# Couples 4 to 8 of an attention and feed-forward kernel: whole filler products, reordered sums, a third place in PSUM

## The chip, the cores and the metric

One core of one Trainium2 chip. The metric is the device time of one execution in microseconds (us). TensorE does the matrix products, VectorE, ScalarE and GpSimd the element-wise work, SyncE issues most of the DMAs.

## The reference

Two blocks follow each other. The first is attention with normalised queries and keys, for 8 batches, 12 heads, 448 rows and a head dimension of 64:

```python
def rmsnorm(x, g):
    rms = np.sqrt(np.mean(x * x, axis=-1, keepdims=True) + 1e-06)
    return x / rms * g
q_n, k_n = (rmsnorm(q, g_q), rmsnorm(k, g_k))
scores = 1.0 / np.sqrt(q.shape[-1]) * np.matmul(q_n, k_n.transpose(0, 1, 3, 2))
scores = scores - np.max(scores, axis=-1, keepdims=True)
attn = np.exp(scores)
attn = attn / (np.sum(attn, axis=-1, keepdims=True) + 1e-09)
attn_out = np.matmul(attn, v)
...
h = x @ w_in
g = h * (1.0 / (1.0 + np.exp(-h)))
out = g @ w_out
```

Between them the heads are brought side by side: x has 3584 rows of 768. w_in is 768 x 2048, w_out 2048 x 768. All is computed in float32; the weights come as 64-bit words that the kernel rounds to float32 itself.

## The kernel before, in words

**Couples.** The attention is done in 24 couples (c = 0 to 23), each of two pairs of heads of one batch; six couples (GROUP) make two batches, whose x is then complete. The loop at L1596 calls visit(c) (L1428) and between(c) (L1504). visit(c) holds the scores of couple c (scores, L726: keys times queries on TensorE in four 64x64 tiles, then the exponential on ScalarE, L740, with the key's factor as its scale), the weighing of the values by the exponentials (weigh, L750), and the division of the couple before (divide, L832). The 448 keys are three full steps (j = 0, 1, 2) of 128 and 64 left over (LEFT). between(c) transposes the next couple's q and k on TensorE (L636, L657; from couple 9 on, VectorE does it, flip, L670), adds the exponentials up (add, L777, on VectorE; sum_up, L790, on TensorE by products with ones), and forms and spreads the reciprocals of the sums (L817 to L828, with two DMAs behind each other for each half).

From couple 6 on, the left-over exponentials of a couple take the place e[1][:, 0] (left_weights, L616), which the first addition add(c, 1) reads.

**Filler products.** The feed-forward block's products are laid into the stretches of the attention in which TensorE would wait. A block of two by two tiles is computed with seven products instead of eight (class Seven, L920). Each product is three matmuls of 128x448 (each of them two passes in the records) that accumulate in one PSUM bank; what follows it (a copy to SBUF on ScalarE, L942 and L952, or a sum on VectorE, L884) takes it out. Products 1 and 2 are in two(), products 6, 5, 7, 3, 4 in five(), in this order. All this is one Python generator that hands over after each matmul, and fill (L1364) draws from it, twice in each between(c): it adds a share of matmuls to filler["due"] and draws until nothing is due, dealing the pieces of other work (`others`: additions, rounding of weights, square sums) evenly between the matmuls, and those of `prompt` (reciprocals and so on) at every third. What follows a product is emitted when the generator is drawn from for the next matmul. The share is 2.4 matmuls in couples 3 to 5 (make_ahead, L973, begun at L1555: 12 matmuls over 5 fills; here the part after a product belongs to the same draw as its last matmul), 13 in couples 6 to 11, 14 after that.

**PSUM.** Eight banks: two single ones named "mm" (used in turn by products, and until couple 5 by sum_up), two tiles of two banks named "sc" (used in turn by each call of scores, by the transposes of q and of k, by sum_up from couple 6 on), and two "av" banks of the weighing. bank (L910) chooses where a product goes: with turns["third"] set and more than 5 matmuls due, every second product goes to an "sc" tile. turns["third"] is set between visit and between for couples from 8 on, and taken back after the first fill up to couple 10 (L1550, L1598).

```python
def bank(n):
    turn = turns["next"] = (turns["next"] + 1) % 4
    if turns["third"] and filler["due"] > 5 * S and not turns["aside"]:
        turns["aside"] = True
        return ps.tile([P, 2, BANK], F32, name="sc", bufs=2)[:, 0, 0:n]
```

**Other work of couples 5 to 7.** normalise(c) (L839) gives pieces: squares of q by ScalarE (L472), their sums by VectorE (L473), the inverse root by VectorE and GpSimd (L497, L501), the scaling of q by GpSimd (L516, at L858), and the same without a scaling for k. Couple 7's q pieces are dealt in couple 5's first fill, its k pieces in visit 6. sum_x (L1005) forms the sums of x that products 5, 6, 4 and 7 need: four steps for each of three parts c; in visit 6 all four steps of the parts 1 and 2 follow the division (L1461 to L1464). The weights are opened by ScalarE (open, L91: L103, L104) and rounded by VectorE and GpSimd (round, L108: L126, L129, L133, L137); sum_w_in (L986) forms the sums of the weights. At couple 10 (FULL, L558) the left-over exponentials are not added by VectorE but given to sum_up as one more term of four matmuls (L801).

**The second matrix.** After the couples, quads of row blocks go through the second product; deep (L1230) again uses seven products, and VectorE and ScalarE combine them.

Of the kernel before, what the change touches and what calls it, by code (L numbers as in the profile page):

```python
# [449 lines left out]
class Norm:  # L450
# [15 lines left out]
    def squares(self, rows, t, out, alone):  # L466
        nc, n = self.nc, out.shape[1]
        t = t[0 : rows.shape[0], 0 : rows.shape[1]]
        if alone:
            nc.vector.tensor_tensor(out=t, in0=rows, in1=rows, op=ALU.mult)  # L470
        else:
            nc.scalar.activation(t, rows, AF.Square)  # L472
        nc.vector.tensor_reduce(  # L473
            out=out, in_=t.rearrange("p (n d) -> p n d", n=n), axis=AX.X, op=ALU.add
        )
# [65 lines left out]
def bounded(  # L541
# [15 lines left out]
    SOON = 2 * GROUP - 1  # L557
    FULL = SOON - 1  # L558

# [230 lines left out]
    def sum_up(c):  # L790
# [8 lines left out]
        if early:  # L799
            terms = [(0, lambda: weights(c, LEFT - 1))] + terms + [(1, None)]  # L800
        if c == FULL:  # L801
            terms.insert(0, (1, None))
# [36 lines left out]
    def normalise(c):  # L839


        def piece(name, i):
            t = scratch[i if c < GROUP + 2 else 0]
            source = raw_of(c) if c < GROUP else q_of(c)
            if name == "q":
                norm.squares_q(c, source, t, i)
            else:
                norm.squares_k(c, place[z.BY_ROWS if c >= LATE else f"k{c % 2}"], t, i)
# [5 lines left out]
            elif i == 1:  # L854
                norm.root(c, name)
                if name == "q":
                    for m in range(2):
# [48 lines left out]
    ps_alone = None  # L906
    turns = dict(next=0, aside=False, third=False)
    filler = dict(work=iter(()), due=0.0, share=0.0)

    def bank(n):  # L910
        turn = turns["next"] = (turns["next"] + 1) % 4
        if turns["third"] and filler["due"] > 5 * S and not turns["aside"]:
            turns["aside"] = True
# [6 lines left out]
    class Seven:  # L920
# [10 lines left out]
        def product(self, name):  # L931
            t, ends = bank(self.n), (self.steps[0], self.steps[-1])
            for s in self.steps:
                nc.tensor.matmul(  # L934
                    t, self.left(name, s), self.right(name, s), start=s == ends[0], stop=s == ends[1]
                )
                if not (self.prompt and s == ends[1]):
                    yield self.n
            return t

        def two(self):
            nc.scalar.copy(self.p1, (yield from self.product("1")))  # L942
            if self.prompt:
                yield self.n
            plus((yield from self.product("2")), self.p1, self.done[1, 1])
            if self.prompt:
                yield self.n

        def five(self):
            p1, u2, u3, p5, done = self.p1, self.u2, self.u3, self.p5, self.done  # L950
            plus((yield from self.product("6")), p1, u2)
            nc.scalar.copy(p5, (yield from self.product("5")))  # L952
            plus((yield from self.product("7")), u2, u3)
            nc.gpsimd.tensor_tensor(out=u2, in0=u2, in1=p5, op=ALU.add)  # L954
            nc.gpsimd.tensor_tensor(out=done[2, 2], in0=u3, in1=p5, op=ALU.add)
            plus((yield from self.product("3")), u2, done[1, 2])
            plus((yield from self.product("4")), u3, done[2, 1])


# [76 lines left out]
    def halves_in(group, blocks, beside=lambda m: iter(()), begun={}, fetched=()):  # L1036
# [11 lines left out]
        for i, m in enumerate(blocks):  # L1048
# [5 lines left out]
            count = 0  # L1054
            for n in columns:
                count += 1
                if (count - 1) % HW == 0:
# [172 lines left out]
    def deep(name, out, more, following, then=lambda t, h: None):  # L1230
# [30 lines left out]
        then(0, 1)  # L1261
        sum_deep_left(following, (0, 1))
        plus(product(7), u2, u3)
        x = added(u3, out[1][0])
        plus(u3, added(p5, out[1][1]), out[1][1])
        then(1, 1)
# [97 lines left out]
    def fill(others=(), prompt=()):  # L1364
# [7 lines left out]
        while filler["due"] > 0:  # L1372
            step = next(filler["work"], None)
            if step is None:
                break
            filler["due"] -= step
            steps += 1
            if prompt and steps % HW == 0:
                prompt.pop(0)()
            while dealt < min(len(others), len(others) * steps // total):  # L1380
                others[dealt]()
                dealt += 1
        filler["due"] = min(filler["due"], 0.0)
        for other in prompt + others[dealt:]:
# [21 lines left out]
    for c in range(GROUP // 2):  # L1406
        halves[2 * (c - GROUP)], halves[2 * (c - GROUP) + 1] = "rr", "o"
    sums_halves = {-6: [(0, 0)], -4: [(0, 1)], -3: [(0, 2)], -2: [(0, 3)]}
    sums_halves[8] = [(3, 0), (3, 1)]
# [18 lines left out]
    def visit(c):  # L1428
# [17 lines left out]
        if c > 0:  # L1446
# [12 lines left out]
            else:  # L1459
                divide(c - 1, sums)  # L1460
                if c == GROUP:  # L1461
                    for steps in (range(2), range(2, 4)):
                        for i in range(1, HW):
                            sum_x(last_two(c), i, steps)  # L1464
                run_all(beside[1:2])
# [38 lines left out]
    def between(c):  # L1504
# [19 lines left out]

        if c == GROUP - 1:
            transposes_and_sums()
        if c < LATE - 1:
# [13 lines left out]
        late = add(c, LEFT - 1) if c >= GROUP else []  # L1541
        if c >= GROUP and c != FULL:
            late += add(c, LEFT)
        further = normalise(c + 2) if c >= GROUP - 1 else []
        late += weights_in(c, 0) + (further[2:] if c >= GROUP else further[:2])
        if LATE - 1 <= c < SOON:
            late.insert(len(late) // 2, lambda: load_q(c + 2))
        fill(late)
        if c < SOON:
            turns["third"] = False  # L1550
        prompt = transposes_and_sums() if GROUP // 2 <= c != GROUP - 1 else []
        if prompt and c < GROUP:
            prompt.insert(0, lambda: None)
        if c == GROUP // 2:
            begin(make_ahead([0, 1]), AHEAD * 2 * HW * S, GROUP - 1)  # L1555
        if c >= LATE - 2:
# [39 lines left out]
    for c in range(NC):  # L1596
        visit(c)
        turns["third"] = c >= LATE - 1  # L1598
        between(c)
    turns["third"] = False  # L1600
    visit(NC)
# [225 lines left out]
```

## Time and profile before

| | us |
|---|---|
| median of 3 runs (1309.18 to 1310.33) | 1309.45 |
| the profiled execution, its own time | 1311.17 |
| its span | 1309.4 |
| TensorE busy in the span | 1291.4 |
| VectorE busy | 951.8 |
| ScalarE busy | 502.7 |
| GpSimd busy | 363.9 |
| TensorE busy of 59 us, 68 to 127 (couples 4, 5, visit 6) | 56.42 |
| TensorE busy of 26 us, 127 to 153 (after visit 6) | 24.54 |
| TensorE busy of 34 us, 153 to 187 (couple 7) | 33.12 |
| TensorE busy of 35 us, 187 to 222 (couple 8) | 33.38 |
| TensorE busy of 40 us, 222 to 262 (couple 9, visit 10) | 39.76 |

The span runs from the first to the last instruction that the profiler recorded. A line of the timeline has the start, the duration from the first start to the last end, the engine, the line of the program, the operation, the names written and read, the shape, and the number of instructions merged. In square brackets stands the idle time of the engine before it and what ended it. A "waits" line has the total, the number of times and the longest. "PE" is TensorE, "DVE" VectorE, "ACT" ScalarE, "POOL" GpSimd; a "q" behind them is the engine's queue, in which DMAs are issued. Ends of matmuls are modelled, and their starts are records: the pace is read from starts.

visit(4) begins at 74.3 us, visit(5) at 96.5, visit(6) at 116.6, visit(7) at 152.2, visit(8) at 187.0, visit(9) at 221.6.

### The profile page before, as it was taken

To read this page: it belongs to the slowest core of one execution; us is meant where nothing else is said; L and a number is where in the kernel's file an instruction comes from. 1 tells how busy PE (TensorE), PEld (TensorE's weight loads), DVE (VectorE), ACT (ScalarE), POOL (GpSimd) and SP (SyncE) were. 2 spreads that over 40 slices of the span, in tenths; PEclk is the share of its full clock that TensorE was granted. 3 is DMA by queue.
4 is the path that set the end of the run, shared out by engine and by line. 5 is a ranking of instruction groups with operands and counts; after the bars stand their busy time and mean duration, and the time that the engine had idled before them with its cause. 6 is when DMAs were issued, how large, how long until landed. Compare 5 with 4: busy or idle time off the path is not lost.

```text
span 1309.4 us, 19898 instructions
## 1 busy us (share of the span) xinstructions
PE 1291.4 (99%) x7178; PEld 828.3 (63%) x7178; DVE 951.8 (73%) x1628; ACT 502.7 (38%) x880; POOL 363.9 (28%) x227
## 2 busy tenths in 40 slices
PE   8999999999999999999999999999999999999998
PEld 4334444444444444444444455558999999999998
DVE  6898767877655556755554786698978787878785
ACT  7866666655544555545544354310000000100000
POOL 6765545453334333334321244300000000000000
PEclk9999999999999999999999999999999999999999
DMA  8675346544444444444321457312323223231411
GB/s 230 167 191 140 93 105 174 144 100 122 97 94 92 123 94 93 99 114 94 86 67 61 142 189 253 125 61 80 105 82 101 90 90 108 71 127 52 135 42 40
DMA packets 267967, 146.32 MB, mean 112 GB/s; under 512 B 204356, under 2 KB 251748, under 8 KB 267860
## 3 DMA queue, kind: packets, MB, share of 16 engines
q1 hardware_dynamic: 267200, 143.80, 40.0%
q8 instruction: 59, 0.97, 0.3%
q0 software_dynamic: 352, 0.96, 0.2%
q14 instruction: 48, 0.39, 0.1%
q10 hardware_dynamic: 308, 0.20, 0.1%
HBM read 95.36 MB, written 41.29 MB: 104 GB/s over the span
## 4 chain that ended last, share of the span: by engine, by line
PE 78%; DVE 2%; ACT 1%; issue 1%; DMA 0%; SPq 0%; ACTq 0%; DVEq 0%
PE alone L1241 23%; PE mm L934 16%; PE sc L934 9%; PE mm L1241 8%; PE alone L934 7%; PE av L772 6%; PE sc L735 6%; PE alone L1278 2%; PE sc L810 1%; PE mm L1278 1%; ACT work L740 0%; DVE work L884 0%; DVE work L786 0%; DVE stage L884 0%; ACT L1579 0%
## 5 line engine op out<-in xcount | busy, mean ns | idle before, releaser
L740 ACT ACTIVATE work<-sc,rms 128x448 f32<-128x448 f32 x318 | 181.3, 634 | 72.9 <-PE sc L735 57.1
L934 PE MATMUL mm<-x,W 128*128 128x448 f32 x396 | 163.4, 546 | 4.7 <-DVE stage L884 1.7
L735 PE MATMUL sc<-work 64*64 64x448 f32 x1344 | 163.8, 544 | 1.4 <-ACT work L740 1.1
L786 DVE TENSOR_TENSOR work<-work 128x896 f32<-128x896 f32 (+1 forms) x112 | 122.5, 1124 | 50.3 <-PE av L772 49.8
L772 PE MATMUL av<-work,rows 64*64 64x448 f32 x1272 | 150.5, 540 | 1.4 <-DVE x L1450 0.9
L934 PE MATMUL mm<-sums_x,W 128*128 128x448 f32 x360 | 147.6, 543 | 1.0 <-DVE parts L884 1.0
L501 POOL TENSOR_TENSOR rms<-rms,minus_half 128x14 f32<-128x14 f32 (+4 forms) x40 | 95.7, 2394 | 135.1 <-DVE rms L497 131.1
L934 PEld LDWEIGHTS mm<-x,W 128*128 128x128 f32 x396 | 72.9, 190 | 85.8 <-issue 70.8
L528 POOL DMA_DIRECT2D out_dram<-x x2 | 1.2, 594 | 443.2 <-DVE x L884 443.2
L934 PEld LDWEIGHTS mm<-sums_x,W 128*128 128x128 f32 x360 | 67.0, 190 | 72.8 <-issue 67.0
L1241 PE MATMUL alone<-W,rows 128*128 128x192 f32 x610 | 113.0, 326 | 0.0
L772 PEld LDWEIGHTS av<-work,rows 64*64 64x64 f32 x1272 | 57.1, 132 | 70.7 <-issue 34.5
L1241 PEld LDWEIGHTS alone<-W,rows 128*128 128x128 f32 x610 | 101.4, 190 | 0.0
L735 PEld LDWEIGHTS sc<-work 64*64 64x64 f32 x1344 | 53.0, 132 | 71.7 <-ACT work L740 29.8
L711 POOL TENSOR_TENSOR rms<-rms,minus_half 128x28 f32<-128x28 f32 x15 | 71.9, 4794 | 67.3 <-DVE rms L708 60.9
L934 PE MATMUL sc<-x,W 128*128 128x448 f32 x216 | 87.9, 543 | 0.0
L954 POOL TENSOR_TENSOR parts<-parts,stage 128x448 f32<-128x448 f32 x31 | 41.5, 1339 | 148.3 <-DVE parts L884 147.9
L1241 PE MATMUL alone<-W,work 128*128 128x192 f32 x382 | 72.2, 326 | 0.0
L934 PEld LDWEIGHTS sc<-x,W 128*128 128x128 f32 x216 | 40.4, 190 | 42.9 <-issue 40.6
L1072 ACT ACTIVATE stage<-stage 128x896 f32<-128x896 f32 x63 | 57.3, 945 | 21.9 <-DVE stage L884 21.0
L1251 ACT COPY rows<-alone 128x192 f32<-128x192 f32 x33 | 10.5, 318 | 141.8 <-PE alone L1241 78.1
L1241 PEld LDWEIGHTS alone<-W,work 128*128 128x128 f32 x382 | 63.8, 190 | 0.0
(261 smaller groups left out, 2282.6 us busy)
## 6 DMA issues: line engine op xcount, KB each, us to landing
hidden<-stage SPq DMA_DIRECT2D x63, 448.0 KB, 3.1
work<-hidden SPq DMA_DIRECT2D x21, 1024.0 KB, 5.2
rows<-in_moe_w_out_dram SPq DMA_DIRECT2D x32, 384.0 KB, 3.3
W<-in_moe_w_in_dram SPq DMA_DIRECT2D x22, 512.0 KB, 5.1
x<-hidden SPq DMA_DIRECT2D x7, 1024.0 KB, 5.7
rows<-in_q_dram SPq DMA_DIRECT2D x120, 56.0 KB, 2.2
rows<-in_k_dram SPq DMA_DIRECT2D x120, 56.0 KB, 2.3
work<-work SPq DMA_DIRECT2D x111, 56.0 KB, 2.0
```

The costliest lines, as they stand in the source:

```text
L501: nc.gpsimd.tensor_tensor(out=t, in0=t, in1=half, op=ALU.pow)
L711: nc.gpsimd.tensor_tensor(out=f, in0=f, in1=minus_half.to_broadcast([P, n]), op=ALU.pow)
L735: nc.tensor.matmul(two[ds(half * D, D), h, 0:S], keys[rows, ts(half, D)], qT[rows, pair, :], start=True, stop=True,)
L740: nc.scalar.activation(left_weights(c)[:, h] if j == LEFT else weights(c, j)[:, i, h], two[:, h, 0:S], AF.Exp, scale=norm.column(c, i, h, j),)
L772: nc.tensor.matmul(sums[i][ds(h * D, D), :], v, w, start=(j == 0 and step == 1), stop=(j == LEFT - 1 and step == 1),)
L786: nc.vector.tensor_tensor(out=total, in0=total, in1=more, op=ALU.add)
L810: nc.tensor.matmul(t[ds(h * D + i * n, n), :], ones[:, which + i if which else 0], left_weights(c)[:, h] if which else w()[:, i, h], start ...
L934: nc.tensor.matmul(t, self.left(name, s), self.right(name, s), start=s == ends[0], stop=s == ends[1])
L954: nc.gpsimd.tensor_tensor(out=u2, in0=u2, in1=p5, op=ALU.add)
L1072: nc.scalar.activation(t, t, AF.Silu)
L1241: nc.tensor.matmul(t, x[:, i], y, start=i == ORDER[0], stop=i == ORDER[-1])
L1278: nc.tensor.matmul(o, a[:, 2 * i + m, t], right_one(name, i)[:, m], start=n == 0, stop=n == len(steps) - 1,)
```

## The change

- **Whole products in couples 3 to 5**: the share becomes 3 matmuls (12 over 4 fills), and couple 5's second fill has none.
- **What follows a product at the end of a fill** is emitted at once, if the fill's last matmul ended a product (filler["ended"]); the generator hands over a 0 after each such part.
- **ScalarE's part of couple 5**: one opening of weights and the two squares of couple 7's q are emitted ahead of the sums and transposes of couple 5; the sums of the squares stay where they were.
- **Couple 7's q** is scaled by VectorE in visit 6, in place of GpSimd.
- **x's sums split**: in visit 6 the parts 1 and 2 have only their first two steps; the third step heads the pieces dealt in couple 6's first fill, the fourth follows the additions and the weights.
- **Couple 6's left-over exponentials** are one more term of sum_up on TensorE; its two additions on VectorE go.
- **Third place**: bank goes by least < due <= most. First fill: over 5 from couple 6 on (before: from couple 8 on). Second fill: over 5 and up to 10 for couples 6 and 7, over 8 for couples 8 to 10 (before: none for these five), over 5 from couple 11 on, as before.
- **deep**: the addition of p5 to the old result moves ahead of product 7's sum.

```diff
@@ -466,7 +466,9 @@
         t = t[0 : rows.shape[0], 0 : rows.shape[1]]
-        if alone:
+        if alone is None:
+            pass
+        elif alone:
             nc.vector.tensor_tensor(out=t, in0=rows, in1=rows, op=ALU.mult)
@@ -555,7 +557,7 @@
     SOON = 2 * GROUP - 1
-    FULL = SOON - 1
+    FULL = (GROUP, SOON - 1)
 
@@ -798,7 +800,7 @@
             terms = [(0, lambda: weights(c, LEFT - 1))] + terms + [(1, None)]
-        if c == FULL:
+        if c in FULL:
             terms.insert(0, (1, None))
@@ -843,7 +845,7 @@
             if name == "q":
-                norm.squares_q(c, source, t, i)
+                norm.squares_q(c, source, t, i, None if c == GROUP + 1 else False)
             else:
@@ -853,7 +855,7 @@
                 norm.root(c, name)
-                if name == "q":
+                if name == "q" and c != GROUP + 1:
                     for m in range(2):
@@ -904,12 +906,13 @@
     ps_alone = None
-    turns = dict(next=0, aside=False, third=False)
-    filler = dict(work=iter(()), due=0.0, share=0.0)
+    turns = dict(next=0, aside=False, least=99, most=99)
+    filler = dict(work=iter(()), due=0.0, share=0.0, ended=False)
 
...
         turn = turns["next"] = (turns["next"] + 1) % 4
-        if turns["third"] and filler["due"] > 5 * S and not turns["aside"]:
+        due = filler["due"] / S
+        if turns["least"] < due <= turns["most"] and not turns["aside"]:
             turns["aside"] = True
@@ -935,26 +938,32 @@
                 if not (self.prompt and s == ends[1]):
+                    filler["ended"] = s == ends[1]
                     yield self.n
+            filler["ended"] = False
             return t
...
         def two(self):
+            rest = self.n if self.prompt else 0
             nc.scalar.copy(self.p1, (yield from self.product("1")))
-            if self.prompt:
-                yield self.n
+            yield rest
             plus((yield from self.product("2")), self.p1, self.done[1, 1])
-            if self.prompt:
-                yield self.n
+            yield rest
 
...
             plus((yield from self.product("6")), p1, u2)
+            yield 0
             nc.scalar.copy(p5, (yield from self.product("5")))
+            yield 0
             plus((yield from self.product("7")), u2, u3)
...
             nc.gpsimd.tensor_tensor(out=done[2, 2], in0=u3, in1=p5, op=ALU.add)
+            yield 0
             plus((yield from self.product("3")), u2, done[1, 2])
+            yield 0
             plus((yield from self.product("4")), u3, done[2, 1])
+            yield 0
 
@@ -1053,6 +1062,9 @@
             for n in columns:
+                if n == 0:
+                    yield n
+                    continue
                 count += 1
@@ -1260,9 +1272,10 @@
         sum_deep_left(following, (0, 1))
+        y = added(p5, out[1][1])
         plus(product(7), u2, u3)
         x = added(u3, out[1][0])
-        plus(u3, added(p5, out[1][1]), out[1][1])
+        plus(u3, y, out[1][1])
         then(1, 1)
@@ -1373,6 +1386,8 @@
                 break
+            if step == 0:
+                continue
             filler["due"] -= step
@@ -1380,6 +1395,8 @@
                 dealt += 1
+        if filler["ended"]:
+            next(filler["work"], None)
         filler["due"] = min(filler["due"], 0.0)
@@ -1405,6 +1422,7 @@
         halves[2 * (c - GROUP)], halves[2 * (c - GROUP) + 1] = "rr", "o"
+    halves[-2] = "r"
     sums_halves = {-6: [(0, 0)], -4: [(0, 1)], -3: [(0, 2)], -2: [(0, 3)]}
@@ -1459,9 +1477,10 @@
                 if c == GROUP:
-                    for steps in (range(2), range(2, 4)):
-                        for i in range(1, HW):
-                            sum_x(last_two(c), i, steps)
+                    for i in range(1, HW):
+                        sum_x(last_two(c), i, range(2))
+                    for i in range(2):
+                        norm.scale(c + 1, q_of(c + 1), q_of(c + 1), i, nc.vector)
                 run_all(beside[1:2])
@@ -1523,6 +1542,11 @@
         if c == GROUP - 1:
+            room.w_in.open()
+            for i, t in enumerate(scratch):
+                size = z.R, 2 * J * D
+                rows = q_of(c + 2)[0 : z.R, ts(i, size[1])]
+                nc.scalar.activation(t[0 : size[0], 0 : size[1]], rows, AF.Square)
             transposes_and_sums()
@@ -1539,20 +1563,29 @@
         late = add(c, LEFT - 1) if c >= GROUP else []
-        if c >= GROUP and c != FULL:
+        if c >= GROUP and c not in FULL:
             late += add(c, LEFT)
         further = normalise(c + 2) if c >= GROUP - 1 else []
-        late += weights_in(c, 0) + (further[2:] if c >= GROUP else further[:2])
+        late += weights_in(c, 0)
+        if c == GROUP:
+            third, fourth = (
+                [lambda i=i, step=step: sum_x(last_two(c), i, (step,)) for i in range(1, HW)]
+                for step in (2, 3)
+            )
+            late = third + late + fourth
+        late += further[2:] if c >= GROUP else further[:2]
         if LATE - 1 <= c < SOON:
...
         fill(late)
-        if c < SOON:
-            turns["third"] = False
+        if GROUP <= c < LATE - 1:
+            turns.update(most=10)
+        elif GROUP <= c < SOON:
+            turns.update(least=8)
         prompt = transposes_and_sums() if GROUP // 2 <= c != GROUP - 1 else []
...
         if c == GROUP // 2:
-            begin(make_ahead([0, 1]), AHEAD * 2 * HW * S, GROUP - 1)
+            begin(make_ahead([0, 1]), AHEAD * 2 * HW * S, AHEAD * 2)
         if c >= LATE - 2:
@@ -1595,9 +1628,9 @@
         visit(c)
-        turns["third"] = c >= LATE - 1
+        turns.update(least=5 if c >= GROUP else 99, most=99)
         between(c)
-    turns["third"] = False
+    turns.update(least=99)
     visit(NC)
```

## The prediction, made before the changed kernel was seen

> **What bounds the kernel now.** I read the page's busy shares, then TensorE's busy time by stretches, then its waits in the stretch that the change touches, then its timeline, and last the timelines of the engines that it waits for.
>
> ```profile
> PE 1291.4 (99%) x7178; PEld 828.3 (63%) x7178; DVE 951.8 (73%) x1628; ACT 502.7 (38%) x880; POOL 363.9 (28%) x227
> ```
>
> TensorE sets the span; it stands still for only 18 us of 1309.4. Of these the last 60 us hold 6.9 and couples 4 to 9 (68 to 262 us) 6.7, which the waits list names in full:
>
> ```profile
> PE mm L934 <- DVE parts L884: 2.6, 4, 0.9
> PE mm L934 <- DVE stage L884: 1.7, 4, 0.7
> PE av L772 <- DVE x L1450: 0.9, 1, 0.9
> PE mm L934 <- ACT stage L942: 0.8, 1, 0.8
> PE mm L934 <- ACT stage L952: 0.6, 1, 0.6
> ```
>
> All but the third are filler products (L934) that wait for a PSUM bank: "mm" has two, and a bank is free only when VectorE or ScalarE has taken its product out. An idle bracket understates a wait: one pass of 128x448 starts 0.376 us after another (2.25 for six in the chain) but ends 0.54 after its own start, and the first one after a pause runs 0.10 longer. So each wait costs its bracket plus 0.27. The wait at 80.77 (0.94 + 0.27 = 1.2, for copies of x) belongs to nothing that the diff touches. The other ten: couple 4 0.99, couple 5 1.08, couple 6 1.22 + 0.79, couple 7 0.89 + 0.53, couple 8 0.86 + 0.77 + 0.80, couple 9 0.51; **8.4 us in all, 0.64%, is the most that the change can take out.** What counts is what ends last in each place once they go.
>
> ```profile
> 94.75 1.77 PE L934 MATMUL mm<-x,W 128*128 128x448 f32 x4 [0.72 <-DVE stage L884]
> 114.14 2.52 PE L934 MATMUL mm<-x,W 128*128 128x448 f32 x6 [0.81 <-ACT stage L942]
> 116.59 0.98 PE L735 MATMUL sc<-work 64*64 64x448 f32 x8
> 122.00 0.93 PE L772 MATMUL av<-work,rows 64*64 64x448 f32 x8
> 128.57 4.69 PE L934 MATMUL mm<-sums_x,W 128*128 128x448 f32 x12
> 134.21 4.78 PE L934 MATMUL mm<-x,W 128*128 128x448 f32 x12 [0.95 <-DVE parts L884]
> 140.36 0.93 PE L665 MATMUL sc<-ident,rows 128*128 128x128 f32 x7
> ```
>
> The two brackets of couples 4 and 5, the start of couple 6's visit (116.59), its first weighing with new banks (122.00), its filler (128.57 to 140.36).
>
> [...] at 123.66 a sum of x took 2.45 us instead of 0.62, beside GpSimd's scaling. [...] the trace has eight passes of L810 on four column tiles every 0.78 us (91.37 to 92.15). [...] here the spread's took 3.6 and 1.9 us, and I use these.
>
> **Couples 4 and 5, whole products.** The 12 matmuls go 3, 3, 3, 3, 0 instead of 3, 2, 3, 2, 2. Every product now ends in its fill, its copy or sum is queued at once, and the bank's next user comes after the sums of weights (some 3 us later): both waits go. Couple 4 loses 0.98 and gains a matmul (2 x 0.376 = 0.75): visit 5 starts 0.23 earlier. Couple 5 loses 1.08 and a matmul: visit 6 starts at 116.59 - 0.23 - 1.83 = **114.5, 2.06 early**. ScalarE's opening and two squares (2 x 0.57 + 2 x 0.52 = 2.2 us) ahead of the transposes cost nothing: its last exponentials end at 108.2 and the q copy waited for TensorE until 111.85, 3.6 us of cover; without it q's and k's copies would be late one for one. In couple 3's second fill an opening now comes behind p1's copy (1.2 us later); VectorE's wait at 80.77 covers it. The store of the last product row is issued before visit 6 in both versions.
>
> **Visit 6: the gain meets a DMA.** VectorE divides couple 5 before weighing couple 6 can take its banks, and the divisors come over three hops:
>
> ```profile
> 114.26 1.22 POOL L826 DMA_DIRECT2D work<-work  x2 [4.09 <-DVE W L126]
> 118.82 0.50 POOL L828 DMA_DIRECT2D work<-work  x1 [3.34 <-DMA work<-work]
> 120.75 1.15 DVE L835 TENSOR_TENSOR x<-av,work 128x448 f32<-128x448 f32 x2 [1.00 <-DMA work<-work]
> ```
>
> The chain starts when TensorE ends couple 5's sums (110.9, now 110.7): two reciprocals of 1.5, GpSimd's two hops, landing at 120.67. None of it is shortened, so the divisions start near 120.5 and the first ends at 121.2. TensorE, 5.41 us after its start, is there at 119.95 and waits 1.2 us. It resumes 0.8 early; the second bank, 0.5 later, staggers the passes as after 80.77 (3.61 for 3.44 us): **0.6 early**. Of 2.06 us, 1.4 are gone.
>
> **Couple 6: the third place meets the exponentials.** From the divisions' end at 121.6, VectorE now has 4 sums instead of 8 (2.4), GpSimd's rounding (L137, behind the power, 123.3 to 124.6) in its way once (1.2; before, GpSimd held it up for 3.0 in all), two scalings of 112x512 (1.1, by 0.69 each at the start of the program, overlapping), two reductions and a root (1.25), the first addition (1.05): it ends at 128.7 instead of 131.6. ScalarE's exponentials of the left-over keys overwrite what this addition reads:
>
> ```profile
> 131.72 1.16 ACT L740 ACTIVATE work<-sc,rms 128x448 f32<-128x448 f32 x2 [4.98 <-DVE work L786]
> ```
>
> so they run from 128.7 to 129.9. The first product (6) has due 13, over 5, and takes an "sc" tile. Seven tiles went to the scores, the eighth to q's transposes; with two buffers the ninth is that of the left-over scores, so product 6 waits for both exponentials. (At the start, 12.64, scores began 0.05 after the second of two exponentials, not after the first.) TensorE is there at 127.97 and starts at **129.9: 1.3 us later than before**. Behind it no wait is left: product 7's tile (q's copy) is free at 130.8, and its sum of x (third step) is queued ahead; fill ends 13 x 0.752 + 0.2 = 9.98 later, at 139.9 against 140.36, 0.46 early. The left-over sums add four matmuls of L810 on TensorE, 0.78 us, and take two additions of 1.1 from VectorE, of which TensorE feels nothing now. **Net 0.3 us late at the second fill.** That had no wait before and has none now. Bounds for product 6's start: 127.97 if exponentials were not in its way (a gain of 1.9) and 131.2 if the scalings meet GpSimd twice (a loss of 1.3).
>
> **Couples 7 and 8: chains that don't shorten.** Banks in a third place let product 7 of couple 7 and product 3 of couple 8 start without their waits. But in couple 7 the fill's last product needs the bank of product 3, whose sum needs GpSimd, FIFO behind rounding and pairing (184.11 to 185.25), behind VectorE's reciprocals and rounding, behind ScalarE's table load and squares, behind the copy at 169.46 that waited for TensorE. The early sum of product 6 moves from between the reciprocals to ahead of them: same total. So that product starts at 185.95 as before, relative to visit 7, and two waits become one of about 1.3. In couple 8 the last product needs the bank of product 4, taken out here, at the end of a VectorE queue with 0.4 us of idle time since 211.4:
>
> ```profile
> 218.36 0.62 DVE L884 TENSOR_TENSOR stage<-mm,parts 128x448 f32<-128x448 f32 x1
> ```
>
> It starts at 219.03 again. The wait at 207.13 has no third place (due 2). **0 of 3.9 us gained.** Couple 9's second fill: product 1 aside lets product 2 start (0.51); product 5 then waits for product 2's sum (252.2): 0.2 gained. Couple 10 had no waits. In later couples a fill ends with a product at 42, 84, 126 and 168 matmuls, always a VectorE sum, at a place with no wait: 0.
>
> **The end.** One 128x192 sum moves ahead; VectorE's last eight operations stand back to back, and only a dependent start (0.38 for 0.28) goes: 0.1 gained.
>
> **Sum.** +0.3 - 0.2 - 0.1 = 0.0. The profiled execution took 1311.17 us, span 1309.4 and 1.8 around it; it stays there, and the median of the runs, 1.7 lower, stays **1309.4**. About 0.2% (2.6 us) is what a measurement can tell from no change.
>
> **Cases.** A, 0.52: as summed, 1308 to 1311.
> B, 0.14: product 6 finds its tile free (127.97): 1.9 less, 1307.5. For it: VectorE has 2.2 us of work less; against: FIFO behind a DMA-bound start.
> C, 0.20: the chains of visit 6 and of couples 7 and 8 shorten as TensorE's waits do. 8.4 less 0.8 gives 1301.8 at most; partly, 1302 to 1306.5. For it: ten brackets out of eleven are aimed at; against: the queues above.
> D, 0.14, slower: the scalings on VectorE wait for GpSimd's power of couple 7's q. GpSimd runs it behind the divisors' last hop and a rounding, from 120.4 to 123.3; VectorE asks at 125.2. If it ends later than that, all behind it, reductions, addition, exponentials, product 6, is late one for one; from 127.8 on the whole is over 2.6 us slower; at 129 it is 1313. Against: 1.9 us of slack.
> Faster by over 0.2% (below 1306.8): C and a quarter of B, 0.24. Slower: most of D, 0.12. Within: 0.64. The range 1304.5 to 1312.0 leaves out the lower half of C and the upper of D; case A's own is 1308 to 1311.
>
> **What would show it.** After: no L934 bracket at couples 4 and 5; visit 6 starting near 114.5; an L772 wait for the division of about 1.2 us near 121; product 6 on "sc" waiting near 2 us for L740; no wait in the rest of that fill; one longer wait at the end of couples 7's and 8's second fills. Wrong if couple 6's filler starts before 128.6, or visit 9 starts over 1 us earlier than before.

## The result, and the profile after

The changed kernel takes **1311.45 us** (median of 20 runs, 1309.83 to 1315.33); the kernel before, beside it, 1309.3 (20 runs, 1308.61 to 1310.33). The ratio is 1.0018, 95% interval 1.0011 to 1.0024: slower by 0.1 to 0.2%, where no change was forecast. (The prediction took 0.2% for the least that can be told from no change; this interval reaches 0.07% to either side.) The profiled execution took 1310.6 us (span 1308.8), one of the quicker of the 20: the median run took 0.85 us more than the one that the trace shows.

The busy line and, for 66 to 262 us, the waits of TensorE in the kernel after (total, times, longest):

```profile
PE 1292.2 (99%) x7186; PEld 831.3 (64%) x7186; DVE 950.7 (73%) x1628; ACT 502.9 (38%) x880; POOL 361.0 (28%) x225
```

```profile
PE mm L937 <- DVE stage L886: 2.5, 2, 1.3
PE av L774 <- DVE x L837: 1.9, 1, 1.9
PE mm L937 <- DVE parts L886: 0.6, 1, 0.6
PE sc L937 <- ACT work L742: 0.5, 1, 0.5
PE sc L737 <- ACT work L685: 0.4, 1, 0.4
PE av L774 <- ACT av L750: 0.3, 1, 0.3
```

Ten waits of filler products have become four, and a weighing (L774) now waits 1.9 us for the division. (Lines have moved: the products are L937, the weighing L774, the division L837.) TensorE's timeline, after:

```profile
110.69 2.42 PE L937 MATMUL mm<-x,W 128*128 128x448 f32 x6
113.03 0.98 PE L737 MATMUL sc<-work 64*64 64x448 f32 x8
...
120.50 1.12 PE L774 MATMUL av<-work,rows 64*64 64x448 f32 x6 [1.88 <-DVE x L837]
...
129.62 2.52 PE L937 MATMUL sc<-sums_x,W 128*128 128x448 f32 x6 [0.50 <-ACT work L742]
...
139.50 0.93 PE L667 MATMUL sc<-ident,rows 128*128 128x128 f32 x7
...
151.97 0.98 PE L737 MATMUL sc<-work 64*64 64x448 f32 x8
...
185.74 1.02 PE L937 MATMUL mm<-x,W 128*128 128x448 f32 x2 [1.16 <-DVE stage L886]
...
218.61 2.52 PE L937 MATMUL mm<-x,W 128*128 128x448 f32 x6 [1.32 <-DVE stage L886]
```

The brackets of couples 4 and 5 are gone. Visit 6 (113.03) stands still at its first weighing; product 6 comes on an "sc" tile, waits for the exponentials, and nothing waits behind it. Couples 7 and 8 end with one wait each. Apart from the sizes, that is the picture that was forecast. What was not forecast is in another view: the stretches of 2 us after that first weighing. The columns are the stretch, the busy times of TensorE, its weight loads, VectorE, ScalarE and GpSimd (instructions in parentheses), then the granted TensorE clock (1.00 is full speed), the DMA share and GB/s.

```profile
120.00:122.00 2.00, 1.50 (x14) 1.01 (x18) 1.97 (x4) 0.61 (x2) 2.00 (x2) 1.00 0.96 208
122.00:124.00 2.00, 2.00 (x16) 1.05 (x12) 1.97 (x3) 0.53 (x1) 0.92 (x1) 0.50 1.09 325
124.00:126.00 2.00, 2.00 (x18) 0.93 (x14) 2.00 (x4) 0.80 (x3) 0.00 (x0) 0.65 0.91 279
126.00:128.00 2.00, 2.00 (x22) 0.76 (x14) 1.97 (x5) 1.16 (x2) 0.85 (x1) 1.00 0.02 4
```

After the pause the clock falls to half, and the pace with it: the two passes of the weighing at 122.10 are followed 0.31 us later, those at 82.33 in the kernel before, at full clock, 0.15 later. By the clock column 1.00 + 0.70 = 1.7 us of TensorE's time are lost (2 us times 0.50 and 0.35) while it counts as fully busy. The fall begins near 122, about 1.5 us after TensorE has resumed. In the kernel before this clock was 1.00 throughout 68 to 262 us; the two stretches there (TensorE's busy time, clock, DMA share and GB/s only):

```profile
122.00:124.00 2.00, 2.00 (x27) 1.00 0.84 181
124.00:126.00 2.00, 2.00 (x24) 1.00 1.14 330
```

A second profile of the kernel before shows that the first was unusual in one wait:

> The kernel before once more, for a second trace of it: visit 7 near 135.6 us after visit 2's start, couple 6's filler without a pause over 1.2 us, clock 1.0 from 20 to 1250 us.

It took 1310.32 us (span 1308.5) instead of 1311.17 (1309.4). Its visits 5, 6 and 7 begin here:

```profile
94.67 0.98 PE L735 MATMUL sc<-work 64*64 64x448 f32 x8
...
114.81 0.98 PE L735 MATMUL sc<-work 64*64 64x448 f32 x8
...
150.29 0.98 PE L735 MATMUL sc<-work 64*64 64x448 f32 x8
```

The wait at 80.77 is not there (in none of the later profiles does it reach 0.3 us), so visits 5 and 6 began 1.8 us ahead of the first profile. The pause and the clock were as expected; the expected 135.6 us from visit 2 to visit 7 were not, they are 109.9. Against this profile, the changed kernel begins visit 6 1.78 us earlier (113.03) and visit 7 1.68 later (151.97 for 150.29): visit 6 and its fillers became 3.46 us longer. All that was won before it, and as much again, is lost there.

### The profile page after: what moved, and what is told of

Read it like the earlier page. It is cut to its first block, busy times and chain, and to the rows that moved or that the text cites. A ratio compares the mean times of both kernels' runs of the same rounds, so it can differ in the third digit from the quotient of the medians.

```text
span 1308.8 us, 19927 instructions
## 1 busy us (share of the span) xinstructions
PE 1292.2 (99%) x7186; PEld 831.3 (64%) x7186; DVE 950.7 (73%) x1628; ACT 502.9 (38%) x880; POOL 361.0 (28%) x225
## 4 chain that ended last, share of the span: by engine, by line
PE 79%; ACT 2%; DVE 1%; DMA 1%; issue 0%; SPq 0%; ACTq 0%; DVEq 0%
PE alone L1253 23%; PE mm L937 15%; PE sc L937 10%; PE mm L1253 8%; PE alone L937 7%; PE av L774 6%; PE sc L737 6%; PE alone L1291 2%; PE sc L812 1%; PE mm L1291 1%; ACT work L742 0%; DVE work L886 0%; ACT L1612 0%; ACT stage L1084 0%; DVE x L886 0%
## 5 line engine op out<-in xcount | busy, mean ns | idle before, releaser
L788 DVE TENSOR_TENSOR work<-work 128x896 f32<-128x896 f32 (+1 forms) x110 | 119.5, 1118 | 50.2 <-PE av L774 49.7
L774 PE MATMUL av<-work,rows 64*64 64x448 f32 x1272 | 153.0, 543 | 2.6 <-DVE x L837 1.9
L937 PE MATMUL mm<-x,W 128*128 128x448 f32 x360 | 148.4, 544 | 3.1 <-DVE stage L886 2.5
L937 PE MATMUL mm<-sums_x,W 128*128 128x448 f32 x342 | 140.6, 543 | 0.0
L937 PEld LDWEIGHTS mm<-x,W 128*128 128x128 f32 x360 | 66.8, 190 | 74.8 <-issue 66.8
L937 PEld LDWEIGHTS mm<-sums_x,W 128*128 128x128 f32 x342 | 63.8, 190 | 68.3 <-issue 64.6
L774 PEld LDWEIGHTS av<-work,rows 64*64 64x64 f32 x1272 | 58.1, 133 | 72.6 <-issue 34.4
L937 PE MATMUL sc<-x,W 128*128 128x448 f32 x252 | 102.5, 543 | 0.0
L937 PEld LDWEIGHTS sc<-x,W 128*128 128x128 f32 x252 | 47.1, 190 | 50.0 <-issue 46.5
```

Source lines behind the costliest of these rows:

```text
L774: nc.tensor.matmul(sums[i][ds(h * D, D), :], v, w, start=(j == 0 and step == 1), stop=(j == LEFT - 1 and step == 1),)
L788: nc.vector.tensor_tensor(out=total, in0=total, in1=more, op=ALU.add)
L937: nc.tensor.matmul(t, self.left(name, s), self.right(name, s), start=s == ends[0], stop=s == ends[1])
```

## The experiments

The theory after the result: the places were read rightly, but each pause was priced by its length alone, at full clock. A pause of TensorE near 2 us (1.88 in this trace) also halves the clock for a while (0.50 here), in a share of the runs. Two rivals: the placement of product 6 alone explains the loss, with the clock as a mere accompaniment; or the load on VectorE does.

### Filling visit 6's pause

```diff
--- after
+        if c == GROUP:
+            awake = ps_mm.tile([P, BANK], F32, name="mm")[:, 0:P]
+            for _ in range(7):
+                nc.tensor.matmul(awake, ident, ident, start=True, stop=True)
         weigh(c, 0, 1)
```

> The changed kernel with seven extra products of 128x128 of the identity, written to a free mm bank, which nothing reads, ahead of couple 6's weighing in visit 6, where TensorE stood still for 1.9 us. They fill most of the pause (some 1.5 us by 0.22 each) and move nothing that waits. Clock theory: the pause itself is behind a DMA and costs the same with or without them, but without them the granted clock fell to 0.5 from 122 to 125 us; with them it stays at 1.0 and the time falls by 1.3 to 1.8 us, from 1311.4 to about 1309.8. Rival (the pause and product 6's wait are the whole loss, the clock's fall is hidden by later waits): unchanged at 1311.4, or slower by what the seven products overrun.

Measured: 1310.16 us (13 runs), ratio to before 1.0005 [0.9997, 1.0014]; the fall of the clock was not avoided, as the theory expected, but moved. TensorE no longer pauses at 120, and the clock is 1.00 there. But now it comes to product 6 on time, and it is that wait which is long. TensorE's timeline of this kernel and its stretches of 5 us:

```profile
128.73 3.92 PE L937 MATMUL sc<-sums_x,W 128*128 128x448 f32 x6 [1.90 <-ACT work L742]
```

```profile
120.00:125.00 5.00, 5.00 (x55) 2.00 (x57) 4.93 (x7) 3.00 (x7) 2.26 (x2) 1.00 0.97 250
125.00:130.00 5.00, 3.10 (x23) 1.61 (x16) 4.46 (x8) 1.95 (x3) 3.35 (x1) 0.97 0.74 223
130.00:135.00 5.00, 5.00 (x10) 2.30 (x9) 2.31 (x3) 0.00 (x0) 0.00 (x0) 0.69 0.01 1
```

Six passes take 3.92 us instead of 2.52. The fall has moved with the pause: 5 x 0.31 + 5 x 0.03 = 1.7 us lost, the same amount at another place. The 13 runs form two groups, seven at 1309.7 to 1310.2 with a mean clock of 0.999, six at 1311.1 to 1312.0 with 0.997 or 0.998; the profiled execution is one of the six.

### Whole products alone

The kernel before with the hand-over of 0, filler["ended"] and the share over AHEAD * 2 = 4 fills, and nothing else of the change. The line that sets the share:

```diff
--- before
-            begin(make_ahead([0, 1]), AHEAD * 2 * HW * S, GROUP - 1)
+            begin(make_ahead([0, 1]), AHEAD * 2 * HW * S, AHEAD * 2)
```

> The kernel before with whole products alone (3 matmuls in each of four fills, what follows a product emitted at a fill's end). Clock theory: TensorE comes to visit 6 two us early and pauses near 2 us for the divisors' DMA; the clock falls there, and the rest of the stretch is as before: slower than before, 1310.0 to 1311.5. Rival (third place or sums in couple 6 make the loss): 0.3 to 0.6 us faster than before, about 1308.8.

Measured: 1310.3 us (13 runs), ratio 1.0002 [0.9993, 1.001]. This lies in the range of the clock theory, but not for its reason: the bracket is 1.19, not near 2, and the profile shows no fall up to 1260 us (a clock of 1.00 throughout). The two waits of couples 4 and 5 go, and by the brackets they come back one for one: 1.19 at the weighing of visit 6, and 1.14 for 0.83 in couple 6's filler. TensorE's timeline of this kernel:

```profile
120.51 1.12 PE L772 MATMUL av<-work,rows 64*64 64x448 f32 x6 [1.19 <-DVE x L835]
...
133.20 4.78 PE L934 MATMUL mm<-x,W 128*128 128x448 f32 x12 [1.14 <-DVE parts L884]
138.50 1.02 PE L934 MATMUL mm<-sums_x,W 128*128 128x448 f32 x2 [0.52 <-DVE parts L884]
```

So this part of the step holds: the gain ahead of visit 6 runs into the division.

### All but the whole products

```diff
--- after
-            begin(make_ahead([0, 1]), AHEAD * 2 * HW * S, AHEAD * 2)
+            begin(make_ahead([0, 1]), AHEAD * 2 * HW * S, GROUP - 1)
```

> The changed kernel with couples 3 to 5 sharing their 12 matmuls over five fills again (3, 2, 3, 2, 2). Clock theory: no pause over 1.3 us in visit 6, clock 1.0 throughout, 1309.0 to 1309.8. Rival (the loss is in couples 6 to 8): stays at 1311 to 1311.5.

Measured: 1311.93 us (21 runs), ratio 1.0015 [1.0008, 1.0022], as slow as the whole change, where the theory expected the loss to go. It had taken visit 6's pause for the only one. The bracket in visit 6 is 0.28; that of product 6 is 1.76. The profiled execution (1310.35, mean clock 0.999) shows no fall up to 1260 us (1.00 throughout), and is one of the group at 1310.0 to 1311.0; 14 of the 21 runs took 1311.5 to 1312.7.

### The third place in couple 6

Two kernels: the change without the third place in couple 6's first fill, and the kernel before with it there.

```diff
--- after
-            turns.update(most=10)
+            turns.update(least=5, most=10)
...
-        turns.update(least=5 if c >= GROUP else 99, most=99)
+        turns.update(least=5 if c > GROUP else 99, most=99)
```

> The changed kernel without a third place in couple 6's first fill. Clock theory: the pause in visit 6 and the fall of the clock stay; product 6 no longer waits for the left-over exponentials (0.5 us in the profile of the changed kernel): 1310.7 to 1311.4. Rival (third place: product 6 behind the exponentials makes the loss): 1309.0 to 1309.8.

```diff
--- before
-        turns["third"] = c >= LATE - 1
+        turns["third"] = c == GROUP or c >= LATE - 1
```

> The kernel before with one part alone: a third place in couple 6's first fill. Product 6 then waits for the exponentials of the left-over keys, which VectorE lets start at 131.7 only: it starts near 133.0 instead of 128.6, 4.4 us later, and the two waits behind it (2.0) go. Place theory: 2.4 us later, and if the clock falls after the pause another 1.0 to 1.7: 1312 to 1314. Rival (a third place does no harm here): 1307.5 to 1309.8.

Measured: without it 1308.6 us (21 runs), ratio 0.9995 [0.9988, 1.0001], 2.9 less than the whole change, and below the ranges of the theory (1310.7 to 1311.4) and of the rival (1309.0 to 1309.8). With it alone 1314.18 (5 runs), ratio 1.0035 [1.0021, 1.0049], the slowest kernel of all. Here is TensorE's timeline of the latter, and its stretches of 5 us:

```profile
131.03 4.85 PE L934 MATMUL sc<-sums_x,W 128*128 128x448 f32 x6 [4.21 <-ACT work L740]
```

```profile
125.00:130.00 5.00, 1.82 (x20) 0.90 (x12) 4.96 (x9) 0.18 (x1) 1.57 (x2) 0.93 0.70 222
130.00:135.00 5.00, 3.97 (x6) 1.92 (x7) 1.72 (x2) 1.78 (x3) 2.14 (x1) 0.50 0.01 3
135.00:140.00 5.00, 5.00 (x13) 2.50 (x12) 4.02 (x5) 1.64 (x4) 0.00 (x0) 0.89 0.00 0
```

Product 6 waits 4.2 us, as VectorE has all its sums of x ahead of the addition, and the clock loses 5 x (0.07 + 0.50 + 0.11) = 3.4 us, twice the 1.7. About 0.9 of these fall into the pause itself (the 0.35 before 130, and half of the 1.03 us up to 131.03), so 2.5 are felt. Two brackets of 0.83 and 0.52 in the same filler are saved: 4.2 + 2.5 - 1.35 = 5.4 us by this sum. Visit 7 begins at 155.14, 4.9 us after that of the second profile of before, and the median is 4.3 higher. So the first rival is right in part: the placement costs by itself, and of all single edits taking it away gains most. But a kernel without it still has the pause at visit 6 and six runs out of 21 at 1310.2 to 1311.3, beside the others at 1307.6 to 1309.5.

### Both together

The last kernel without third place in couple 6's first fill, and with visit 6's pause filled by the seven products of the first experiment.

> The changed kernel without a third place in couple 6's first fill and with the seven idle products in visit 6's pause, so that neither pause is left. Clock theory with both pauses: the clock stays up in all runs; times lie close together at 1307.5 to 1308.3, without the group of runs near 1310.5 that the kernel without the third place alone had. Rival (that group comes from elsewhere): median 1308.6 or over, and a third of the runs still near 1310.5.

Measured: **1307.85 us** (21 runs, 1307.18 to 1309.14), ratio 0.9985 [0.9979, 0.9992]: faster than both kernels. TensorE's stretches of 5 us and its waits for 66 to 262 us:

```profile
120.00:125.00 5.00, 5.00 (x54) 2.22 (x56) 4.93 (x7) 3.12 (x7) 2.71 (x2) 1.00 0.97 253
125.00:130.00 5.00, 5.00 (x29) 2.63 (x22) 4.97 (x9) 2.01 (x4) 3.06 (x1) 1.00 0.74 228
```

```profile
PE mm L937 <- DVE stage L886: 2.3, 2, 1.2
PE mm L937 <- DVE parts L886: 0.7, 1, 0.7
PE sc L737 <- ACT work L685: 0.4, 1, 0.4
PE av L774 <- ACT av L750: 0.2, 1, 0.2
```

TensorE doesn't stand still between 100 and 145 us; visit 7 begins at 149.11. The upper group of runs is gone, though seven products were added. That is the cleanest separation of length and clock: filling visit 6's pause shortens no chain (visit 6 takes 35.9 us to visit 7 here and 36.0 in the profile without the filling), and the upper group disappears with it. VectorE's work is the same in both, so its load doesn't make the upper group. Nor does the chip: on the same one, the next kernel has an upper group.

### Moving matmuls instead of filling the pause

The kernel without third place in couple 6's first fill, with couple 4's second share of three matmuls given to couple 5's second fill.

```diff
+            share = filler["share"]
+            if c == GROUP - 2:
+                filler["share"] = 0.0
             fill(weights_in(c, 1) + (further[:2] if c >= GROUP else []), prompt)
+            filler["share"] = share
```

> The changed kernel without a third place in couple 6's first fill, and with whole products 3, 3, 0, 3, 3 over the fills of couples 3, 4, 4, 5, 5 instead of 3, 3, 3, 3, 0: three matmuls stand behind couple 5's sums instead of ahead of them, so the divisors' chain starts earlier and TensorE has 2.3 us more to do beside it. Chain theory (the pause in visit 6 is set by the chain from the sums of couple 5): no pause over 0.5 us in visit 6, 1306.3 to 1307.5. Rival (VectorE or the DMAs before it hold the chain where it is): the pause only moves, 1308 to 1309.

Measured: 1308.05 us (13 runs), ratio 0.9993 [0.9985, 1.0001]. Visit 6 begins at 114.14, finds the division done, and has no pause; visit 7 begins at 148.38, 0.7 earlier than with the filled pause. A wait of 1.08 comes up at visit 5 for copies of x, and the last wait of couple 8 is 1.61 (1.16 with the filled pause). The pause of visit 6 went as expected, but not the time (1306.3 to 1307.5). Eight runs took 1307.3 to 1309.0, five 1310.1 to 1310.6. Which pause was to blame for these five was open, so the next kernel takes away the longest.

### The third place in the second fills

```diff
--- the kernel with moved matmuls
-        if GROUP <= c < LATE - 1:
-            turns.update(least=5, most=10)
-        elif GROUP <= c < SOON:
-            turns.update(least=8)
+        if GROUP <= c < SOON:
+            turns.update(least=99)
```

> The kernel with the shifted products (whole products 3, 3, 0, 3, 3; no third place in couple 6's first fill), and without the third place in the second fills of couples 6 to 10, so that the one merged wait at the end of couple 7's and of couple 8's second fill (1.3 and 1.8 us) is again two of 0.4 to 1.4. Theory (a pause of TensorE of about 1.5 us or more lets the granted clock fall in a share of the runs, and each such fall costs some 1.7 us more): the runs near 1310.5 of the shifted kernel become rare, median 1307.3 to 1308.0. Rival (the clock falls from the pause of 1.2 us at visit 5, or from nothing that the pauses set): as many runs near 1310.5 as before, about 4 in 10. Rival (the third place in the second fills earns its waits in full): 1309 to 1310, slower than the shifted kernel by the waits of couples 6 to 9.

Measured: **1307.87 us** (21 runs, 1307.05 to 1308.86), ratio 0.9988 [0.9981, 0.9995]. The upper group is gone. TensorE's timeline in couples 7 and 8:

```profile
182.21 1.02 PE L937 MATMUL mm<-x,W 128*128 128x448 f32 x2 [1.16 <-DVE stage L886]
...
203.38 1.77 PE L937 MATMUL mm<-x,W 128*128 128x448 f32 x4 [0.58 <-DVE parts L886]
...
209.41 2.52 PE L937 MATMUL mm<-sums_x,W 128*128 128x448 f32 x6 [0.16 <-DVE parts L886]
...
214.94 2.52 PE L937 MATMUL mm<-x,W 128*128 128x448 f32 x6 [0.52 <-DVE stage L886]
```

Couple 8's one wait of 1.61 is two of 0.16 and 0.52 again, couple 7's is the same 1.16, and that of visit 5 is still 1.08. So the wait of 1.61 us is the one that goes with the five upper runs, though no profile shows a fall at it; those of 1.16 and 1.08 stay, and the runs are of one group. The third place in these fills earned nothing: visits 7 to 9 take 69.09 us without it and 69.50 with it.

### The left-over sums on VectorE again

```diff
--- the kernel with the filled pause and no third place in couple 6's first fill
-    FULL = (GROUP, SOON - 1)
+    FULL = (SOON - 1,)
```

> The kernel kept awake ahead of visit 6, without third place in couple 6's first fill, with couple 6's left-over exponentials added by VectorE again (two additions of 1.1 us; four products with ones less on TensorE, 0.78 us). The step as predicted (TensorE pays 0.78 us, VectorE's relief isn't felt): 0.5 to 0.8 us faster than with the change's way, 1307.0 to 1307.4. Rival (VectorE's 2.2 us are felt in couple 6's fills now that they begin 2 to 3 us earlier): waits of some 1 us come back between 127 and 150 us, 1307.9 to 1309.

Measured: 1308.36 us (13 runs), ratio 0.9992 [0.9984, 1.0001]: slower than with the sums on TensorE (1307.85), though the two intervals overlap; this is what the rival expected. TensorE's timeline of this kernel has the reason:

```profile
136.78 1.02 PE L937 MATMUL mm<-sums_x,W 128*128 128x448 f32 x2 [0.78 <-DVE parts L886]
...
216.20 2.52 PE L937 MATMUL mm<-x,W 128*128 128x448 f32 x6 [1.53 <-DVE stage L886]
```

The first wait does not exist with the sums on TensorE, and its bracket is as long as they take (0.78). Visit 7 begins at 149.35 instead of 149.11, and visit 9 at 218.79 instead of 218.25, as the second wait is 1.53 for 1.16.

## Why the prediction was wrong

**The step that failed is the price of a pause.** "Each wait costs its bracket plus 0.27", and the whole sum, took TensorE at full clock on both sides. The prediction moved 1.2 us of waiting to visit 6 and 1.9 to product 6 and booked them as 3.1 us; it never asked what a pause that long does to the clock. In the profile the pause at visit 6 cost 1.88 us and then 1.7 more by the clock (0.50 and 0.65 from 122 to 126 us). Of the 20 runs of the changed kernel, 16 have a mean clock of 0.998 or less; of the 123 runs of the kernel before that ran beside the experiments, six. The profile of before held one warning: the clock was 1.00 up to 1250 us and 0.97 in the last 60, where it is 0.52 from 1306 to 1308, some 3 us after TensorE's last product (it ends at 1303.2).

The table orders the kernels by the longest bracket in the profiled execution between 66 and 262 us. The runs were not all traced, so at which pause an untraced one lost its clock isn't seen. The mean clock is a rough sign: it holds the end of the span too, where no product is left for a fall to delay (from 1303.2 us on in the first profile of before). The profiled run with the pause filled and no third place in 6 has 0.998 with a clock of 1.00 in every stretch from 20 to 1250 us and 0.97 from 1250 to 1305; and one fall of 1.7 us alone is 0.0013 of the span, so a run with 0.999 can have had one. The last column counts the runs of an upper group by their times, where a gap sets one apart.

| kernel | longest bracket, us | mean clock 0.998 or less | upper group by time |
|---|---|---|---|
| pause filled, no third place in 6 | 1.16 | 2 of 21 | 0 |
| matmuls moved, no third place in second fills | 1.16 | 2 of 21 | 0 |
| whole products alone | 1.19 | 2 of 13 | 0 |
| before (second profile) | 1.24 | 6 of 123 | 2 (1311.3, 1312.3) |
| no third place in 6 | 1.30 | 8 of 21 | 6 |
| left-over sums on VectorE | 1.53 | 1 of 13 | 1 |
| matmuls moved | 1.61 | 5 of 13 | 5 |
| all but whole products | 1.76 | 11 of 21 | 14 |
| after | 1.88 | 16 of 20 | no gap |
| after, visit 6's pause filled | 1.90 | 6 of 13 | 6 |
| before, third place in 6 | 4.21 | 5 of 5 | no gap |

Below 1.3 us there is hardly an upper run; above, the share is large but in no strict order (1.53 and 1.90 stand out of it), as a single traced execution doesn't fix the length of the other runs' pauses. Falls were traced only at brackets of 1.88, 1.90 and 4.21.

**The sum, mended.** The four runs of the changed kernel at clock 0.999 took 1309.83 to 1311.86, in the middle 1310.4; with visit 6's pause filled, the seven runs at 0.999 1310.0. By this estimate 0.6 to 1.0 us over the forecast come at full clock, and about 1 to 1.4 from falls in most runs. It is rough, as 0.999 doesn't rule out a fall.

- **Couples 4 and 5**: right. Forecast 2.06 us, measured 1.78 against the second profile, which lacks the wait at 80.77. ScalarE's moved work cost nothing that shows.
- **Visit 6**: right place, mis-sized. Forecast a wait of 1.2; its bracket is 1.88 (1.19 in the kernel with whole products alone). The chain of the divisors did not shorten, as forecast; it grew. GpSimd's and VectorE's lines of the kernel after:

```profile
112.56 1.22 POOL L828 DMA_DIRECT2D work<-work  x2 [3.29 <-DVE W L126]
...
116.77 0.50 POOL L830 DMA_DIRECT2D work<-work  x1 [2.99 <-DMA work<-work]
116.88 1.99 DVE L129 TENSOR_SCALAR W<-W 128x512 int32<-128x512 int32 x1
117.28 1.30 POOL L137 TENSOR_TENSOR W<-W 128x512 int32<-128x512 int32 x1
...
118.91 0.69 DVE L133 SCALAR_TENSOR_TENSOR W<-W 128x512 int32<-128x512 int32 x1
...
119.82 1.16 DVE L837 TENSOR_TENSOR x<-av,work 128x448 f32<-128x448 f32 x2 [0.22 <-DMA work<-work]
```

From the issue of the last hop (116.77) to the division (119.82) it is 3.05 us, where 1.93 was measured before; what made it longer isn't shown. And VectorE would hardly have been ready: its rounding (L129) falls beside GpSimd's work and takes 1.99 us instead of 0.43. In the kernel without the third place in couple 6, a rounding of VectorE beside GpSimd's (1.99 for 0.69) was what the division followed, and no DMA; with whole products alone it is the same (L497, 1.62 for 0.17). The prediction took VectorE's queue as free here, since it had 1.0 us of idle time before.

- **Product 6**: right. Forecast 1.9 us of waiting for both exponentials; brackets of 1.76 and 1.90 in the two kernels in which TensorE came on time. In the profiled execution of the changed kernel only 0.50 is left, as the pause and the slow clock had held TensorE up already. There the exponentials followed TensorE's own scores and not VectorE's addition:

```profile
128.41 1.16 ACT L742 ACTIVATE work<-sc,rms 128x448 f32<-128x448 f32 x2 [1.14 <-PE sc L737]
```

So its start at 129.62, where 129.9 was forecast, agrees by luck: TensorE came to visit 6 1.5 us earlier than forecast, as the wait at 80.77 was missing, and lost that and more in the longer pause and to the clock.
- **Left-over sums**: half right. They cost TensorE the 0.78, but "TensorE feels nothing now" of VectorE's relief was wrong: without it a wait of 0.78 us comes back in couple 6's filler. The pair is worth about 0.5 us to the kernel by the medians (0.9 by the two ratios), an estimate, as the intervals overlap.
- **Couples 7 and 8**: right. In each, waits became one longer wait, and the time is the same: visits 7 to 9 take 69.23 us after, 69.43 before.
- **Couple 9 and the end**: forecast 0.3 gained together. Visits 9 to 10 take 32.47 for 32.51 us; from visit 10 to the end 1055.1 for 1055.3. Too small to tell.
- **The rivals**: B (product 6 finds its tile free) is ruled out by the brackets. D (the scalings wait for GpSimd's power) did not come: the power ends at 121.66, the scalings begin at 124.51 right behind their forerunner. C came true in part only where product 6 was given its "mm" bank back and visit 6's pause was removed: 1.6 to 2.0 us in the medians, of the 8.4 aimed at.

What lowers the clock isn't shown; the runs show the pauses, the falls and their sizes. In the traces the clock falls to half (0.50), with 1.7 us lost in two of them (brackets of 1.88 and 1.90 us) and 3.4 in the third (4.21). That a pause brings the fall on is a reading of these three, and of the upper group of runs that is gone once visit 6's pause is filled (6 of 21 runs, then none).

## What to carry to other kernels

On a kernel whose TensorE is busy 99% of the time, price a pause in two parts: its length, and, where it nears 2 us (1.88 and 1.90 here), the risk of some 1.7 us more at half the clock. Where that risk begins isn't settled: upper groups of runs appeared from a traced bracket of 1.3 us on, traced falls from 1.9. Short waits that are gathered into one long wait can therefore cost more than they did apart, at the same sum; and a bank that is free "somewhere" is worth taking only if its last reader is early. Compare a second profile of the kernel before, and the spread of the runs with the mean clock of each, before a difference of 0.1 to 0.2% is explained by a single trace.

## What the runs showed of the hardware that was not expected

- A pause of TensorE of 1.88 us was followed by a clock of 0.50, then 1.00 again, with 1.7 us lost; at one of 4.21 us the clock lost 3.4. After TensorE's last product, too, the clock fell to half (0.52 from 1306 to 1308 in the first profile of before). Brackets of up to 1.76 us were followed by no fall in the traced executions, though in kernels with a traced bracket of 1.30 us or more a share of the other runs has a lower mean clock.
- The mean clock differs from run to run of one kernel, and the time with it. With matmuls moved, eight runs took 1307.3 to 1309.0 us at 0.999 or 1.000 and five 1310.1 to 1310.6 at 0.997 or 0.998.
- VectorE's rounding with one input (L129, 128x512) took 1.99 us beside GpSimd's rounding (L137) in the kernel after, and 0.43 without it in the kernel before (118.05).
- The last hop of the divisors from SBUF to SBUF took 1.93 us in the first profile of before and 3.05 in that of after, from its issue to the division behind it, with the same 56 KB.
